# Blocks 8 to 11 normalised in place by GpSimd and transformed in the head; GpSimd issues the stores of x1; last output stores split another way

## The chip, the cores and the metric

The kernel runs on one core of a Trainium2 chip. The core has five engines, each with an instruction stream of its own: TensorE (PE, matmuls; its weight loads are listed as PEld), VectorE (DVE), ScalarE (ACT), GpSimd (POOL) and SyncE (SP, which issues transfers). [...] ACT, SP and POOL issue transfers (DMAs). The metric is the device time of one execution in microseconds; the median of several executions is given.

## The reference, cut to what matters

Two branches are applied to the same normalised input and added to the raw input.

```python
x  = A_u                                   # (1, 2048, 448)
xn = (x - mean(x)) / sqrt(var(x) + 1e-5)   # over the 448 channels
# branch A: a state-space model as a long convolution
dt = exp(log_dt);  A = -exp(log_A_real) + 1j*A_imag;  C = (C_real + 1j*C_imag)*dt
K[d, l] = 2 * Re( sum_n C[d, n] * exp(A[d, n]*dt[d]*l) )     # N = 256, l < 2048
yA = irfft(rfft(K, 4096) * rfft(xn, 4096))[:2048] + xn * D_skip
# branch B: a gated linear unit
yB = (sigmoid(xn @ w_gate) * (xn @ w_up)) @ w_down           # F = 1792
out = x + yA + yB
```

Everything is float32. The kernel writes the matmuls of branch B as three matmuls of rounded parts (high*high, low*high, high*low).

## The kernel before, in words

The 2048 tokens are 16 blocks of 128 tokens (blocks 0 to 7 are the first half, 8 to 15 the second); the 448 channels lie in the free dimension. Two generators write the program: `conv` for branch A and `glu` for branch B. A loop at the end advances whichever is less far, by the estimates in `total`. What they write gets priorities, and when the program is built a scheduler fixes the order on each engine from the dependences, the priorities and its own estimate of when each operand will be there. So a changed line can move instructions far from it. On the chip the order stands.

`conv` has three stages.

1. **Head.** `x_stats` and `x_scales` find mean and inverse root of the variance. `x_scales(sm, 8, 8)` does so for blocks 8 to 15, as a chain of ten small DVE instructions (128x8) after the first guess `ys`. `x_norm` normalises a block. Blocks 0 to 7 are loaded, normalised and transposed at once for the GLU. `x_spec` takes two normalised blocks through the **first Fourier stage**: small matmuls by `wx` (L280) fill three banks of PSUM, `tr`, `ko` and `kp`, which exist once each; three ACT copies (L293 for `tr`, L295 for `ko` and for `kp`) take them to two of three tiles `x1a`, `x1b`, `x1c`, and four DMAs (L300) store these to `x1_d` in DRAM. A bank can be filled again when its copy is done, and a tile when its two DMAs have landed. Beside this `prep` works out the pole parameters from the weights (long DVE and ACT chains, L303 to L430), and the GLU's first feature tiles run.
2. **Kernel spectrum** (`kgen`). For 56 chunks of 8 channels POOL builds magnitudes by doubling (`me`, `mf`, L508 and L520), ACT builds sines `S` (L548 to L551), DVE multiplies them (`Et`, `Ft`, L602 to L604) and PE contracts them (`ko`, L616). A second small transform (L566) stores the spectrum to `sk_d`.
3. **Spectra** (`spectra`). It reads `x1_d` and `sk_d` back, multiplies, transforms back (L902, L929, L962) and adds into the output accumulators; `out` stores these.

`glu` runs the gate and up matmuls (L709), the gate function (`th` on ACT L717, `hf` on DVE L720, `hh` L725, `hl` L727) and the down matmuls (`po`, L825, with the DVE sum L830). It treats blocks 0 to 7 first (half 0) and 8 to 15 after (half 1). PSUM tiles with the tag `gu` exist four times and serve gates, down sums and more. In the last group of half 0, the **cross** stage, the second half's blocks are loaded once more in pairs (`pair_load`); `pair_norm` normalises a pair, `pair_turn` transposes it for the GLU (L213), and `pair_first` puts it through the first Fourier stage: four `gu` banks, four ACT copies (L689), four DMAs on ACT's queue (L691). The table `mid` says which step runs between the two matmul groups of the cross stage's four gates, `end` what follows each gate, and `downs` what follows a down sum:

```python
mid = [(pair_norm, 8), None, (pair_first, 8), (pair_first, 10)]
downs = {(0, 0): (pair_first, 12), (0, 1): (pair_turn, 14), (0, 3): (pair_first, 14)}
```

In the head the second half's blocks also lie in SBUF, raw, in the tiles `xes` (`xe0` for blocks 8 to 11, `xe1` for 12 to 15); before, they serve only `x_stats`, and the space of `xe0` then becomes `p01`.

## Time and profile before

| what | value |
|---|---|
| three timed runs | 711.12, 714.69, 714.64 us |
| median | 714.64 us |
| profiled execution | 710.54 us |
| its span, first to last instruction | 708.8 us |
| mean granted TensorE clock in it | 0.988 |
| PE busy | 668.1 us (94%) |
| DVE, ACT, POOL busy | 555.7, 428.7, 384.9 us |
| DMA traffic | 117.22 MB |

A row of a timeline is: start in us from the span's start, duration in us, engine, line of the kernel, operation, output<-inputs, tile shape, count; in brackets the idle time of that engine just before, and which instruction ended it. ACTq and SPq rows are DMA issues on those queues. A row of a table by stretches gives, for a stretch of time, the busy time of each engine in it, then the granted clock (1.00 is full), the mean busy share of the 16 DMA engines and GB/s.

### The profile page before, as it was taken

To read this page: it belongs to the slowest core of one execution; us is meant where nothing else is said; L and a number is where in the kernel's file an instruction comes from. 1 tells how busy PE (TensorE), PEld (TensorE's weight loads), DVE (VectorE), ACT (ScalarE), POOL (GpSimd) and SP (SyncE) were. 2 spreads that over 40 slices of the span, in tenths; PEclk is the share of its full clock that TensorE was granted. 3 is DMA by queue.
4 is the path that set the end of the run, shared out by engine and by line. 5 is a ranking of instruction groups with operands and counts; after the bars stand their busy time and mean duration, and the time that the engine had idled before them with its cause. 6 is when DMAs were issued, how large, how long until landed. Compare 5 with 4: busy or idle time off the path is not lost. (4 is left out here: it accounts for less than half of the span.)

```text
span 708.8 us, 19098 instructions
## 1 busy us (share of the span) xinstructions
PE 668.1 (94%) x7752; PEld 523.7 (74%) x7752; DVE 555.7 (78%) x766; ACT 428.7 (60%) x678; POOL 384.9 (54%) x433
## 2 busy tenths in 40 slices
PE   2798999999999998999999999999999999999996
PEld 2575878878877875756878878877777777777784
DVE  5899987699899998898478899988946555566544
ACT  3656965578689779877577788778543322322320
POOL 2101227655999999777446698798765001344001
PEclk9999999999999998989999999999999999999999
DMA  9956274554253544546833333242269988999756
GB/s 200 239 149 204 70 230 150 170 183 132 63 169 135 169 123 135 162 146 202 258 112 103 92 112 108 68 138 82 54 179 280 257 236 238 266 272 221 182 146 182
DMA packets 93031, 117.22 MB, mean 165 GB/s; under 512 B 12240, under 2 KB 76624, under 8 KB 92944
## 3 DMA queue, kind: packets, MB, share of 16 engines
q1 hardware_dynamic: 65376, 91.75, 46.3%
q10 hardware_dynamic: 24896, 18.13, 8.7%
q0 software_dynamic: 2672, 6.13, 3.2%
q8 instruction: 61, 1.00, 0.6%
q14 instruction: 26, 0.21, 0.1%
HBM read 72.13 MB, written 43.84 MB: 164 GB/s over the span
## 5 line engine op out<-in xcount | busy, mean ns | idle before, releaser
L520 POOL TENSOR_TENSOR me<-me,pm 128x32 f32<-128x32 f32 (+1 forms) x168 | 154.9, 922 | 66.8 <-DVE Et L603 38.1
L520 POOL TENSOR_TENSOR mf<-mf,pm 128x64 f32<-128x64 f32 (+1 forms) x112 | 116.9, 1044 | 5.1
L709 PE MATMUL gu<-xh,wh 128*128 128x512 f32 x336 | 100.1, 405 | 3.8 <-DVE acc L830 1.6
L709 PE MATMUL gu<-xh,wl 128*128 128x512 f32 x336 | 96.9, 393 | 0.0
L709 PE MATMUL gu<-xl,wh 128*128 128x512 f32 x336 | 95.1, 390 | 0.0
L602 DVE TENSOR_TENSOR Et<-me,S 128x1024 f32<-128x1024 f32 x56 | 80.2, 1433 | 11.6 <-ACT S L551 10.3
L825 PE MATMUL po<-dh,hh 128*128 128x448 f32 x224 | 84.2, 376 | 3.1 <-ACT hh L725 1.9
L548 ACT ACTIVATE S<-tr 128x1024 f32<-128x1024 f32 x56 | 57.7, 1030 | 44.9 <-PE tr L542 41.0
L604 DVE TENSOR_TENSOR Ft<-mf,S 128x1024 f32<-128x1024 f32 x56 | 80.1, 1431 | 5.3 <-PE ko L616 3.7
L603 DVE TENSOR_TENSOR Et<-me,S 128x1024 f32<-128x1024 f32 x56 | 80.4, 1436 | 4.8 <-ACT me L533 4.5
L825 PE MATMUL po<-dh,hl 128*128 128x448 f32 x224 | 82.4, 369 | 0.3 <-DVE hl L727 0.3
L825 PE MATMUL po<-dl,hh 128*128 128x448 f32 x224 | 82.3, 368 | 0.0
L709 PEld LDWEIGHTS gu<-xh,wh 128*128 128x128 f32 x336 | 60.8, 189 | 24.2 <-issue 4.4
L709 PEld LDWEIGHTS gu<-xh,wl 128*128 128x128 f32 x336 | 63.4, 189 | 14.7 <-DVE ve L255 0.7
L709 PEld LDWEIGHTS gu<-xl,wh 128*128 128x128 f32 x336 | 63.0, 188 | 13.5
L725 ACT CAST hh<-hf 128x512 fp32r<-128x512 f32 x56 | 34.9, 623 | 62.4 <-DVE hf L720 61.4
L616 PEld LDWEIGHTS ko<-Et,Ft 128*32 128x32 f32 x3584 | 54.7, 112 | 24.2 <-issue 13.4
L720 DVE SCALAR_TENSOR_TENSOR hf<-th,gu 128x512 f32<-128x512 f32 x56 | 38.1, 680 | 39.9 <-PE gu L709 35.2
L786 POOL TENSOR_TENSOR dl<-rd,dh 128x448 fp32r<-128x448 f32 x14 | 25.6, 1830 | 78.8 <-ACT dh L785 68.5
L616 PE MATMUL ko<-Et,Ft 128*32 128x64 f32 x3584 | 65.2, 223 | 2.6 <-DVE Ft L604 2.4
L551 ACT ACTIVATE S<-S,hpi 128x1024 f32<-128x1024 f32 x56 | 65.5, 1170 | 0.0
L717 ACT ACTIVATE th<-gu 128x512 f32<-128x512 f32 x56 | 33.5, 599 | 49.4 <-PE gu L709 43.0
(208 smaller groups left out, 1318.0 us busy)
## 6 DMA issues: line engine op xcount, KB each, us to landing
sk_d<-sk ACTq DMA_DIRECT2D x14, 512.0 KB
sx<-x_d SPq DMA_DIRECT2D x32, 224.0 KB
skl<-sk_d SPq DMA_DIRECT2D x16, 448.0 KB
vp<-v_d SPq DMA_DIRECT2D x16, 448.0 KB
v_d<-vt SPq DMA_DIRECT2D x14, 448.0 KB
ph<-ph_d SPq DMA_DIRECT2D x224, 24.0 KB
wt_d<-wh SPq DMA_DIRECT2D x9, 512.0 KB
wt_d<-wl SPq DMA_DIRECT2D x9, 512.0 KB
```

The costliest lines, as they stand in the source:

```text
L520: ins = nc.gpsimd.tensor_tensor(m[:, :, w + a : 2 * w : n], m[:, :, a:w:n], par(base + i).unsqueeze(2).to_broadcast([128, 4 * DC, w // n]) ...
L548: nc.scalar.activation(rows(cs), pv, AF.Abs)
L551: sins[:] = [nc.scalar.activation(cs, cs, AF.Sin, scale=-TWO_PI, bias=hpi)]
L602: v.tensor_tensor(Et[:, :, :, 32:64], two(me[:, :, 32:64]), S[:, 1::-1], ALU.mult)
L603: v.tensor_tensor(Et[:, :, :, 0:32], two(me[:, :, 0:32]), S[:, 1:3, :, ::-1], ALU.mult)
L604: fts[:] = [v.tensor_tensor(Ft, two(mf), S[:, 3:5], ALU.mult)]
L616: mm = nc.tensor.matmul(ko[32 * j : 32 * j + 32, sl], Ft[:, cc, DC * h + 4 * q + j], Et[:, cc, DC * h + 4 * q + j], start=(k == 0), stop=( ...
L709: glu_mm[:] = [nc.tensor.matmul(ps, a_, b_, start=(n == 0), stop=(n == len(mm) - 1))]
L717: marks[0] = nc.scalar.activation(th, pgu[0], AF.Tanh, scale=0.5)
L720: marks[1] = v.scalar_tensor_tensor(hf, th, 1.0, pgu[1], ALU.add, ALU.mult)
L725: nc.scalar.copy(hh, hf)
L825: glu_mm[:] = [nc.tensor.matmul(po, a_[:, bs], w_, start=(n == 0), stop=(n == 3 * fc - 1))]
```

## The change

- `x_scales` for blocks 8 to 15: after the first guess the remaining steps run on POOL, as 14 instructions of 128x8, instead of ten on DVE.
- Four POOL instructions (L1088 of the new kernel) then normalise blocks 8 to 11 in place in `xe0`, and two further calls of `x_spec` in the head take them through the first Fourier stage. `p01` takes over the space of `xe0` only after that. The estimate `total` grows by 8.
- `pair_first` for blocks 8 and 10 goes from the cross stage. The pairs are still loaded, normalised and transposed there, for the GLU.
- All stores to `x1_d` (24 DMAs in the head, 8 in the cross stage, 32 as before) are issued by POOL instead of ACT.
- At the end: blocks 12 and 13 are stored in two column halves, the first by POOL before the last stretch; the last stores carry blocks 14 and 15 instead of 15 alone.

```diff
@@ x_scales
+        if b0 >= 8:
+            for _ in range(3):
+                nc.gpsimd.tensor_tensor(z[:, b], y, y, ALU.mult)
+                nc.gpsimd.tensor_tensor(z[:, b], z[:, b], ve[:, b], ALU.mult)
+                nc.gpsimd.tensor_scalar(z[:, b], z[:, b], -0.5, 1.5, ALU.mult, ALU.add)
+                nc.gpsimd.tensor_tensor(y, y, z[:, b], ALU.mult)
+            nc.gpsimd.tensor_tensor(z[:, b], mv[:, b, 0], y, ALU.mult)
+            nc.gpsimd.tensor_scalar(zs[:, b0 : b0 + nb], z[:, b], -1.0, None, ALU.mult)
+            return
@@ x_spec
-                nc.scalar.dma_start(to.rearrange("g i k d -> (i k) g d"), x1s_[p][:, :, H * h : H * h + H])
+                nc.gpsimd.dma_start(to.rearrange("g i k d -> (i k) g d"), x1s_[p][:, :, H * h : H * h + H])
@@ pair_first
-            nc.scalar.dma_start(
+            nc.gpsimd.dma_start(
                 x1_d[:, r : r + 2].rearrange("h i k d -> (i k) h d"), to.rearrange("p (h d) -> p h d", h=2)
@@ glu
-                    mid = [(pair_norm, 8), None, (pair_first, 8), (pair_first, 10)]
+                    mid = [(pair_norm, 8), None, None, None]
...
-                                out(accs[3], 12, 3, slice(0, D), (nc.sync, nc.scalar))
+                                out(accs[3], 12, 2, slice(H, D), (nc.sync, nc.scalar))
...
+                        if final and (t, b) == (1, 1):
+                            out(acc, 12, 2, slice(0, H), (nc.gpsimd,))
...
-                        out(acc, 15, 1, slice(0, D), (nc.sync, nc.scalar))
+                        out(acc, 14, 2, slice(0, D), (nc.sync, nc.scalar))
@@ conv
-                p01 = pst.tile([CP, 2, 2, 2 * N], F32R, name="p01", tag="xe0")
-                for i in range(2):
-                    slots[f"P{i}"] = p01[:, i]
+                for b in range(8, 12):
+                    xe = xes[0][:, b % 4]
+                    nc.gpsimd.tensor_scalar(xe, xe, ys[:, b : b + 1], zs[:, b : b + 1], ALU.mult, ALU.add)
...
+                    if n in (4, 5):
+                        yield from x_spec([xes[0][:, 2 * (n - 4) + i] for i in range(2)], 2 * n)
+                    if n == 5:
+                        p01 = pst.tile([CP, 2, 2, 2 * N], F32R, name="p01", tag="xe0")
@@ the loop that interleaves
-    total = [sum(Y0) + 11 * WP + 8 * WX + 34 + NCK * WK + HOLE + 17 * WS, 2 * (4 + NFT * 14.8) - HELD]
+    total = [sum(Y0) + 11 * WP + 12 * WX + 34 + NCK * WK + HOLE + 17 * WS, 2 * (4 + NFT * 14.8) - HELD]
```

Lines of the new kernel stand 7 lower in the middle (L293, L295, L300 become L300, L302, L307; L709 becomes L716, L825 L832) and up to 16 lower at the end.

POOL in the head, after the load of `sel`: before, two of the GLU's small subtractions `dl` stand there with nothing between them.

```order
L1064 DMA sel<-in_c_sel_dram 128x512
L786 TENSOR_TENSOR dl<-rd,dh 128x448 x2
L584 MEMSET pm_1167 128x128
```

Now (the number behind a name tells tiles of one kind apart) the end of the scale chain, the stores, a `dl` and the four normalisations follow each other there.

```order
L307 DMA x1_d_59<-x1c_480 128x2x224 x2
L261 TENSOR_SCALAR z_87<-z_87 128x8
L307 DMA x1_d_59<-x1ab_383 128x2x224 x2
L262 TENSOR_TENSOR ys_79<-ys_79,z_87 128x8
L793 TENSOR_TENSOR dl_625<-rd_623,dh_622 128x448
L263 TENSOR_TENSOR z_87<-mv_85,ys_79 128x8
L264 TENSOR_SCALAR zs_80<-z_87 128x8
L1088 TENSOR_SCALAR xe0_116<-xe0_116,ys_79,zs_80 128x448 x4
L307 DMA x1_d_59<-x1ab_383 128x2x224 x2
L307 DMA x1_d_59<-x1c_480 128x2x224 x2
```

The stores of the third `x_spec` (the last two rows) now come after the four normalisations, and those of the second in the middle of the chain.

PE in the head: in the new kernel the sixth `x_spec` (`xe0` by `wx`) stands between the last down sum `po` and the next gate, and the order on ACT leads up to the copy of the bank `kp` that the fifth one left (`kp_765`).

```order
L287 MATMUL tr_831<-xe0_116,wx_68 64x448 x4
L287 MATMUL ko_832<-xe0_116,wx_68 64x448 x2
L287 MATMUL kp_833<-xe0_116,wx_68 64x448 x2
L716 MATMUL gu_862<-xh_94,wh_849 128x512 x3
```

```order
L300 COPY x1c_480<-tr_763 128x896
L385 ACT_TABLE_LOAD
L385 ACTIVATE junk_81<-w3_399 112x1
L302 COPY x1ab_383<-ko_764 128x448
L367 ACTIVATE fr_390<-aim_149,hdt_392 112x256 x2
L394 ACTIVATE m3_386<-w3_387,qpi_75 112x512
L395 ACTIVATE s3_388<-w3_387,qpi_75 112x512
L403 CAST ki_389<-fr_390 112x512
L394 ACTIVATE m3_398<-w3_399,qpi_75 112x512
L395 ACTIVATE s3_400<-w3_399,qpi_75 112x512
L302 COPY x1ab_383<-kp_765 128x448
```

Three copies have been put among the activations of `prep`, and the copy of `kp_765` stands behind seven of them; `kp_833` cannot be written before it.

PE in the cross stage, where pair 8 passes its first stage: before,

```order
L542 MATMUL tr<-sel,ph_1112 128x512 x2
L280 MATMUL gu<-xt,wx 64x448 x2
L616 MATMUL ko<-Et_1105,Ft 32x64 x32
L280 MATMUL gu<-xt,wx 64x448 x4
L213 MATMUL gu<-ident,xt 64x128 x2
L542 MATMUL tr<-sel,ph_1112 128x512 x2
L280 MATMUL gu<-xt,wx 64x448 x2
```

and now

```order
L623 MATMUL ko<-Et_1186,Ft 32x64 x27
L716 MATMUL gu<-xl,wh 128x512 x3
L716 MATMUL gu<-xh,wh 128x512 x3
L716 MATMUL gu<-xr,wh 128x512
L716 MATMUL gu<-xh,wl 128x512 x3
L716 MATMUL gu<-xr,wl 128x512
L716 MATMUL gu<-xl,wh 128x512 x3
```

The four groups of small matmuls are gone and gate matmuls follow the chunk directly. Over the whole program the first chunk of `ko` now stands behind 22 more matmuls of the GLU, and the spectra stage begins behind 11 more.

More of the change, by code (lines that the diff above doesn't have):

```diff
@@ L260, in x_scales @@
             v.scalar_tensor_tensor(y, z[:, b], 1.5, y, ALU.add, ALU.mult)
-        neg = lim[:, b0 // 4, 0:1] if b0 < 8 else -1.0
-        v.scalar_tensor_tensor(zs[:, b0 : b0 + nb], mv[:, b, 0], neg, y, ALU.mult, ALU.mult)
-        if b0 < 8:
-            limits(b0 // 4)
+        v.scalar_tensor_tensor(zs[:, b0 : b0 + nb], mv[:, b, 0], lim[:, b0 // 4, 0:1], y, ALU.mult, ALU.mult)
+        limits(b0 // 4)
     def x_norm(xn, xt, b):
@@ L1097, in conv @@
                             yield from x_spec([xns[n - 2][:, b + i] for i in range(2)], 4 * (n - 2) + b)
+                    if n in (4, 5):
+                        yield from x_spec([xes[0][:, 2 * (n - 4) + i] for i in range(2)], 2 * n)
+                    if n == 5:
+                        p01 = pst.tile([CP, 2, 2, 2 * N], F32R, name="p01", tag="xe0")
+                        for i in range(2):
+                            slots[f"P{i}"] = p01[:, i]
             with tc.tile_pool(name="pk", bufs=1, side="right", reuse_waits="tile") as pk:
```

## The prediction

> **What bounds the kernel now.** I read the page first (busy time by engine, granted clock in 40 slices), then a table of busy time by stretches, then groups, waits and timelines of the two stretches that the change touches.

> ```profile
> PE 668.1 (94%) x7752; PEld 523.7 (74%) x7752; DVE 555.7 (78%) x766; ACT 428.7 (60%) x678; POOL 384.9 (54%) x433
> PEclk9999999999999998989999999999999999999999
> 40.00:77.00 37.00, 33.61 (x197) 25.24 (x196) 36.44 (x74) 24.65 (x49) 2.44 (x2) 1.00 0.59 177
> 200.00:270.00 70.00, 67.21 (x1058) 54.62 (x1058) 69.17 (x68) 57.44 (x83) 68.03 (x62) 1.00 0.53 158
> 270.00:290.00 20.00, 18.00 (x243) 11.14 (x241) 16.28 (x18) 17.78 (x30) 18.28 (x20) 0.83 0.43 127
> 290.00:330.00 40.00, 37.31 (x532) 23.68 (x522) 37.05 (x44) 33.80 (x56) 29.88 (x34) 0.91 0.48 152
> 520.00:702.00 182.00, 180.59 (x1553) 137.82 (x1551) 99.05 (x191) 48.74 (x92) 41.57 (x53) 1.00 0.84 226
> ```

> PE is the bound: 668.1 of 708.8 us. Only two things can move the time much: gaps on PE (about 41 us in all) and stretches in which PE runs at a lower clock. From 520 to 702 PE is idle for 1.4 us, so whatever the change shifts there is worth nothing until the last store. The touched places are the head (40 to 77, PE idle 3.4 us, DVE 36.44 of 37) and the cross stage (270 to 330, PE idle 4.7 us, granted clock 0.83 and 0.91). In the 70 us ahead of the cross stage DVE works 69.17 us.

> **Cross stage: what goes.** The groups of PE in 270:290 and 290:300, the clock in steps of 5 us, and two rows of ACT:

> ```profile
> L280 PE MATMUL gu<-xt,wx 32*64 32x448 f32 x16 | 4.7, 663 | 2.0 <-DVE xl L220 1.3 <-DVE hf L720 0.7
> L280 PE MATMUL gu<-xt,wx 32*64 32x448 f32 x16 | 2.0, 560 | 0.0
> 275.00:280.00 5.00, 3.75 (x74) 1.53 (x62) 5.00 (x6) 5.00 (x9) 4.92 (x4) 0.93 0.15 49
> 280.00:285.00 5.00, 5.00 (x73) 3.15 (x73) 3.38 (x3) 5.00 (x9) 4.84 (x7) 0.50 0.56 177
> 285.00:290.00 5.00, 5.00 (x79) 3.79 (x77) 2.90 (x5) 3.24 (x6) 3.83 (x6) 0.89 0.47 142
> 310.00:315.00 5.00, 5.00 (x53) 2.91 (x53) 4.96 (x6) 5.00 (x9) 4.69 (x5) 0.50 0.42 128
> 315.00:320.00 5.00, 5.00 (x71) 3.83 (x70) 4.65 (x6) 3.83 (x7) 0.27 (x2) 0.82 0.27 92
> 301.98 2.77 ACTq L691 DMA_DIRECT2D x_d<-x  x2
> 304.79 0.58 ACT L219 CAST xh<-gu 128x512 fp32r<-128x512 f32 x1 [2.41 <-issue]
> ```

> - Pair 8 takes 4.7 us of PE, pair 10 2.0: 6.7 us of matmul go.
> - Pair 8 waits 2.0 us for free `gu` banks (the releasers are DVE's `xl` and `hf`). These waits go with it, unless DVE is itself the limit.
> - The clock: after these small, waiting matmuls it is 0.93, 0.50 and 0.89 in three steps of 5 us, a loss of (0.07 + 0.50 + 0.11) x 5 = 3.4 us. Some 0.9 of it is already in the 4.7 (the last group of pair 8 took 1.75 us instead of 0.97 in the timeline), so 2.5 us more. I take it as gone, since pair 8's stalls precede it. A second such stretch (310 to 320, again (0.50 + 0.18) x 5 = 3.4 us) follows pair 12's first stage, which stays; I leave it.
> - Sum: 6.7 + 2.0 + 2.5 = 11.2 us at the most. Against it stands DVE: in 270 to 330 it is busy 16.28 + 37.05 = 53.3 of 60 us, so if every step there needs DVE, no more than its idle 6.7 us can go. If DVE's backlog from before 270 carries on, still less: 0 to 3. I take **−8** (0 to −11): above DVE's 6.7 because part of the removed matmuls stood where PE, not DVE, was full (280 to 290, DVE 6.28 of 10).
> - ACT's two store issues at 301.98 took 2.77 us and left ACT 2.41 us without work; these go to POOL, which is idle 10 us in 290 to 330 and gets eight issues. With one more row,

> ```profile
> L239 POOL DMA_DIRECT2D out_dram<-ac x8: 551/551/563, 639.1 to 643.0; - x8
> ```

> eight at 0.55 are 4.4 us: hidden, if no `me`/`mf` step that DVE waits for is behind them. Price without that cover: 4.4 us. I count 0.

> **Head: what comes.** PE at full width, ACT, and the nearest POOL rows:

> ```profile
> 41.02 0.60 PE L280 MATMUL tr<-xn,wx 32*64 32x448 f32 x4
> 41.96 0.96 PE L709 MATMUL gu<-xh,wh 128*128 128x512 f32 x3
> 76.81 0.86 PE L709 MATMUL gu<-xh,wh 128*128 128x512 f32 x3
> 46.63 1.20 SPq L642 DMA_DIRECT2D wraw<-in_B_w_up_dram  x2
> 50.71 1.05 ACT L759 CAST wh<-wraw 128x1024 fp32r<-128x1024 f32 x1 [1.11 <-DMA wraw<-in_B_w_up_dram]
> 62.85 1.19 SPq L642 DMA_DIRECT2D wraw<-in_B_w_up_dram  x2
> 66.03 0.89 ACT L293 COPY x1ab<-tr 128x896 f32<-128x896 f32 x1
> 68.90 0.53 ACT L295 COPY x1ab<-ko 128x448 f32<-128x448 f32 x1
> 79.83 0.71 ACT L388 ACTIVATE s<-w,qpi 112x512 f32<-112x512 f32 x1
> 80.45 0.61 ACT L396 CAST ki<-fr 112x512 int32<-112x512 f32 x1
> ```

> An `x_spec` costs PE 0.94 us (41.02 to 41.96, sixteen matmuls side by side), so two cost 1.9 us. But the sixth stands in front of the gates that started at 76.81, and its bank `kp` is free only when ACT has copied the fifth's. On ACT that copy now stands just behind the last `prep` activation, which ended at 80.45. To that time come: a third wide copy (0.8), two narrow ones (0.95), a cast that now stands earlier (0.5), so 82.7 less 0.5 that starts overlap = 82.2. Two waits are ahead of it on the same engine. A cast of the next weights `wh` has been moved ahead of the activations; its load is issued at 62.85, and the earlier such load was cast 4.1 us after its issue (46.63 to 50.71, with 1.11 us of waiting), so it can start near 66.95: about 0.9 us of waiting. And the copies into the tile `x1ab` wait for the stores of its last content, which POOL issues only after the four normalisations: about 0.7. So the copy starts near 83.8, ends near 84.3, and the gates start near 84.5 instead of 76.81: **+7.7**. Without the waits it is +6.1. If the activations run earlier than I think, because ACT is ahead, only the matmuls stay: +1.9. All prices of the normalisation hang on POOL:

> ```profile
> 47.38 0.17 DVE L256 TENSOR_SCALAR ys<-ve 128x8 int32<-128x8 int32 x1
> 112.88 0.32 POOL L508 TENSOR_TENSOR mf<-GG,pm 128x64 f32<-128x64 f32 x1
> 119.23 1.29 POOL L520 TENSOR_TENSOR mf<-mf,pm 128x64 f32<-128x64 f32 x1
> 84.11 4.41 POOL L786 TENSOR_TENSOR dl<-rd,dh 128x448 fp32r<-128x448 f32 x1 [24.74 <-ACT dh L785]
> L793 POOL CAST dh<-rdw x5: 551/552/791, 513.1 to 643.5; 128x448 fp32r<-128x448 f32 x5
> ```

> The trace has no 128x8 instruction of POOL. The nearest are 128x64: 0.32 us alone and 1.29 beside a busy DVE. Fourteen are 4.5 to 18.1 us; I take 0.6 each, 8.4, since DVE's instructions in the head are mostly shorter than the `Et` that runs beside the 1.29. The four normalisations have one tensor operand, as the cast of the same shape has (0.55), so 2.2 us, and at most 4 x 4.41 = 17.6 by the two-operand `dl`. With twelve issues ahead of them (6.6) POOL's share is some 17 us from 47.4 on, done near 65 to 70. The fifth and sixth stages are then not late, as the gates in question come after 76. DVE is spared ten instructions of about 0.1 us, 1 us; it is full here, but PE waits for ACT, so 0.

> [...]

> [...]

> ```profile
> 35.35 0.50 PE L709 MATMUL gu<-xr,wh 128*128 128x512 f32 x1 [2.53 <-DVE xr L226]
> 61.25 0.47 PE L825 MATMUL po<-dh,hh 128*128 128x448 f32 x1 [1.85 <-ACT hh L725]
> ```

> The longest gaps of the head, 2.53 and 1.85 us, left the clock at 1.00. The new one is longer: 7.7 − 1.9 leaves 5.8 us of idle PE, of which some 1.5 to 2 lies ahead, where copies of the fifth stage hold PE too, so 3.7 to 4.4 in one piece. I leave its clock out of the forecast and put it into the slow rival.

> **Tail.**

> ```profile
> L239 SPq DMA_DIRECT2D out_dram<-acc x6: 316/674/980, 701.1 to 704.6; - x6
> 699.41 2.21 DVE L970 TENSOR_TENSOR acc<-acc,pv 128x448 f32<-128x448 f32 x4 [0.34 <-PE pv L962]
> 702.00:709.00 7.00, 0.09 (x1) 0.00 (x0) 0.62 (x1) 0.00 (x0) 0.00 (x0) 0.78 0.66 196
> ```

> After the last matmul six issues on SP's queue and six on ACT's put out 7 us x 196 GB/s = 1.37 MB. Half of blocks 12 and 13 (2 x 128 x 224 x 4 bytes = 0.23 MB) now leaves earlier: 0.23 MB at 196 GB/s is 1.2 us at most, and nothing if the last blocks' own landing sets the end. I take **−0.7**. The early half is issued by POOL, 0.55 us; POOL is busy 41.6 of 182 us there, so it is hidden.

> The spectra's later start (11 more matmuls ahead of them) changes no sum while PE is busy 180.59 of 182 us. Price if they starve: the 11 matmuls by 0.4 us, 4.4.

> **Sum.** 710.54 + 7.7 − 8 − 0.7 = 709.5. The profiled execution lies 0.6 us under the lowest of the three runs and 4.1 under their median; two runs stand at 714.7 and one at 711.1, a step of 3.5 us, as large as one of the clock losses above. A changed kernel may show either level; I add 1: **710.5 us**. Against the median of 714.64 that is faster by 0.6%, at the edge of what a measurement of this kernel can tell from no change (about 0.5%, 3.6 us).

> **Rivals.**

> 1. *The head costs more: POOL's chain is late (718).* If DVE holds POOL up in each of the fourteen small steps, as at 119.23, the stores of tile `x1c`, which POOL issues behind ten of them, are reached at 47.4 + 10 x 1.29 = 60.3.

> ```profile
> rdw<-in_B_w_down_dram POOLq DMA_DIRECT2D x5, 224.0 KB, 4.3
> 60.58 0.62 ACT L725 CAST hh<-hf 128x512 fp32r<-128x512 f32 x1 [2.64 <-DVE hf L720]
> ```

> Two issues (1.1) and a landing as that of `rdw`, which POOL issues too (4.3), make 65.7. ACT's copy of the third stage (0.9) waits for that tile, and the `hh` behind it starts near 66.8 to 67.2 instead of 60.58, 6.6 later. ACT's two waits of the forecast (1.6) and some 1.2 of its other idle time (12.3 of 37 us) take up 2.8 of that: the head costs 7.7 + 3.8 = 11.5, and the gap on PE, over 4 us, lowers the clock: 3.4 more. 710.5 − 7.7 + 11.5 + 3.4 = 717.7. It decides from 0.65 us a step: 60.4, where ACT needs the tile, less 47.6, 1.1, 4.3 and 0.9 leaves 6.5 for ten. For it: DVE is 98% busy in 40 to 77. Against: its instructions there differ from those beside the 1.29.
> 2. *The cross stage gives all (704.5).* The whole 11.2, the second clock loss too (half of 3.4) and no waits in the head (+6.1): 711.5 + 6.1 − 11.2 − 1.7 − 0.7 = 704. For it: both clock losses follow a first stage that waits, and DVE has idle time after 280. Against: DVE is full before 275, and pair 12 stays.
> 3. *The change gives nothing there.* DVE is the limit of the cross stage, the gain there is 3, the head floor 6.1: 711.5 + 6.1 − 3 − 0.7 = 713.9, no difference.

> **How the numbers follow.** Forecast 0.45, its own range 707 to 714 (the gain between 6.7 and 10, the head between 6.1 and 9); the slow head 0.22, the full gain 0.25, the third 0.08. Half of the forecast's case lies under 711.1, which is faster by over 0.5%: 0.45 x 0.46 + 0.25 = 0.46 faster. Over 718.2 is most of the slow head and a little of the rest: 0.19. The remaining 0.35 is within. The range, 703 to 719, takes in the full gain and the slow head, and leaves out both clock losses gone with a free head, and a slow head with a full DVE.

> **What would show it.** In the profile of the changed kernel: the gates after the sixth `x_spec` start near 84.5, with a wait of `kp` for ACT's copy of 3.7 to 4.4 us ahead; POOL's fourteen steps take 0.3 to 0.65 us each; the clock is 1.00 from 275 to 290 (times shifted by the head); PE's groups in the cross stage hold 32 matmuls of L287 fewer; the last store lands some 5 us after PE's last matmul. It is wrong if `kp` waits under 2 us, if a clock step follows it, if the cross stage of the new kernel takes as long as before, or if PE waits there for POOL.

## The result, and the profile after

The changed kernel takes **733.71 us** (median of five: 737.20, 732.91, 732.34, 733.71, 734.04), the kernel before 712.79 (five, 710.22 to 714.69). The ratio is 1.0299, with an interval of 1.0269 to 1.0330: 3% slower, where the prediction had 710.5 and a range up to 719. The profiled execution of the changed kernel is the 737.20 one, with a span of 735.4 us; before it was 708.8. The two profiled executions thus lie 26.6 us apart, the medians 20.9: nearly 6 us of what the traces below add up to are this pair's own spread.

The same two lines of the page as before, then the table of busy time by stretches:

```profile
PE 679.0 (92%) x7752; PEld 532.5 (72%) x7752; DVE 568.3 (77%) x756; ACT 428.3 (58%) x676; POOL 414.9 (56%) x487
PEclk9998899999998999998999999999999999999999
40.00:77.00 37.00, 35.15 (x188) 23.54 (x188) 35.61 (x64) 21.51 (x46) 28.13 (x36) 0.91 0.53 169
77.00:100.00 23.00, 20.23 (x91) 14.95 (x90) 18.90 (x31) 20.17 (x38) 7.59 (x9) 0.85 0.49 153
200.00:270.00 70.00, 63.15 (x919) 51.41 (x918) 57.52 (x61) 51.02 (x73) 53.36 (x55) 0.95 0.43 134
300.00:350.00 50.00, 40.58 (x616) 27.78 (x613) 44.62 (x49) 37.85 (x60) 43.22 (x55) 0.90 0.44 134
350.00:540.00 190.00, 181.45 (x2747) 148.28 (x2749) 167.74 (x161) 135.23 (x194) 148.71 (x158) 0.98 0.36 107
540.00:726.00 186.00, 183.83 (x1684) 140.97 (x1681) 104.24 (x191) 53.74 (x99) 43.98 (x57) 0.99 0.82 221
```

PE has the same number of matmuls, 10.9 us more busy time and 15.7 us more idle time; together that is the 26.6 us by which the spans differ. The added busy time is not added work: weighting each slice's busy time with its granted clock gives 662.3 us of work at full clock, against 661.3 before. So some 16 us went to gaps and 10 us to half clock; the 1 us more of work is within the error of this weighting.

That weighting also gives a ruler. If the busy time times the clock is added up along each trace, both kernels can be compared at the same amount of PE work done. The table shows how many us later than the kernel before a kernel reaches that point (all worked out from slices of 2.5 us, one trace for each kernel; the last three rows are experiments, told below):

| PE work done (us) | 40 | 90 | 190 | 210 | 250 | 270 | 310 | 330 | 470 | 650 |
|---|---|---|---|---|---|---|---|---|---|---|
| time of the kernel before | 57 | 111 | 212 | 233 | 275 | 299 | 346 | 366 | 509 | 691 |
| changed kernel | −0.1 | +6.6 | +6.2 | +13.2 | +13.1 | +13.3 | +15.8 | +16.0 | +24.3 | +26.5 |
| changed, interleaved as before | +2.2 | +5.2 | +5.0 | +5.4 | +5.9 | +3.0 | +7.5 | +10.9 | +10.1 | +10.7 |
| the same, accumulator loads later | +0.2 | +6.5 | +6.2 | +5.4 | +5.7 | +3.1 | +6.2 | +6.2 | +5.3 | +6.1 |
| before, with the new `total` alone | 0.0 | +0.2 | +0.4 | +6.0 | +8.3 | +8.4 | +6.9 | +6.9 | +9.7 | +11.9 |

The changed kernel loses 6.6 us in the head, 7 us in one piece between 220 and 246 us of its own time, 3 over the cross stage, 8 in the second half of the kernel spectrum, and 2 in the spectra. (The +2.2 in the second kernel's first column is half clock from 34.2 to 41.0 us, behind 2.08 us of idle time from 30.8 to 34.2, ahead of the steps that were added; see the last section.) Only the first of these stands in the sum of the prediction.

**The head.** Waiting PE rows, ACT's copy that releases one of them, and the chain on POOL:

```profile
60.91 0.73 PE L287 MATMUL ko<-xn,wx 32*64 32x448 f32 x2 [1.85 <-ACT x1c L302]
85.71 1.76 PE L287 MATMUL kp<-xe,wx 32*64 32x448 f32 x4 [2.77 <-ACT x1ab L302]
85.14 0.51 ACT L302 COPY x1ab<-kp 128x448 f32<-128x448 f32 x1
48.01 5.48 POOL L261 TENSOR_SCALAR z<-z 128x8 f32<-128x8 f32 x1
54.42 1.28 POOL L261 TENSOR_SCALAR z<-z 128x8 f32<-128x8 f32 x1
56.82 1.49 POOL L307 DMA_DIRECT2D x_d<-x1c  x2 [0.28 <-issue]
64.25 3.62 POOL L1088 TENSOR_SCALAR xe<-xe,ys,zs 128x448 f32<-128x448 f32 x4
60.00:65.00 5.00, 4.09 (x13) 2.28 (x14) 5.00 (x7) 2.29 (x8) 4.78 (x6) 0.62 0.62 197
85.00:90.00 5.00, 4.29 (x10) 2.41 (x11) 4.39 (x8) 4.94 (x10) 1.63 (x3) 0.51 0.30 97
```

`kp` waits for ACT's copy as foreseen, and the third stage's `ko` waits for a copy whose tile `x1c` is stored from the middle of POOL's chain, which is the slow rival's place. But the idle time of the head grew by 0.4 us only; the rest, some 6.2 us, is half clock, 6.8 us long each, behind these two gaps.

**The stall near 226 us.** Rows of POOL, SP, ACT and PE in order of time:

```profile
221.39 5.78 POOL L527 TENSOR_TENSOR mf<-mf,pm 128x64 f32<-128x64 f32 x4
227.13 1.19 POOL L793 TENSOR_TENSOR dl<-rd,dh 128x448 fp32r<-128x448 f32 x1
228.34 0.34 SPq L796 DMA_DIRECT2D dt_d<-dl  x1
229.26 3.33 SPq L499 DMA_DIRECT2D ph<-ph_d  x8
231.59 0.40 ACTq L581 DMA_DIRECT2D sk_d<-sk  x1
232.09 1.02 ACT L555 ACTIVATE S<-tr 128x1024 f32<-128x1024 f32 x1 [9.81 <-DMA ph<-ph_d]
234.57 1.22 PE L549 MATMUL tr<-sel,ph 128*128 128x512 f32 x2 [6.27 <-ACT S L557]
```

ACT's copies of `sk` are done at 222.3, and the store of `sk` is issued at 231.6. Why it waits for a load of `ph`, which has nothing to do with it, is seen in the program's order with its waits (SP's first `ph` load, and ACT's store):

```
L499 DMA ph1_1194<-ph_d_58 12x2x256 [waits DMAHW2_49,PE_49]
L581 DMA sk_d_60<-sk_1181 128x8x128 [waits DMAHW2_49,Activation_49]
```

In this program the transfers of SP and ACT take eight semaphores in turn (in the trace, the numbers 100, 101 and 110 to 115), and by the waits listed with them one that takes a semaphore again waits until its last user has landed. The store's last user is a `ph` load that SP issues behind the store of `dl`, at 229.26, 2.33 us ahead of the store; `dl` stands on POOL behind 5.8 us of `mf`. Nothing behind the store runs on ACT in these 9.81 us. So GpSimd holds up SP, SP holds up ACT, ACT holds up PE, which stands 6.27 us.

**The tail.** PE's last matmul started at 729.21 of 735.4 us, before at 701.72 of 708.8; with 0.37 us for each, 5.8 us follow it instead of 6.7.

### The profile page after: what moved, and what is told of

Its sections match the earlier page's. It is cut to its first block, busy times and chain, and to the rows that moved or that the text cites. A ratio compares the mean times of both kernels' runs of the same rounds, so it can differ in the third digit from the quotient of the medians.

```text
span 735.4 us, 19134 instructions
## 1 busy us (share of the span) xinstructions
PE 679.0 (92%) x7752; PEld 532.5 (72%) x7752; DVE 568.3 (77%) x756; ACT 428.3 (58%) x676; POOL 414.9 (56%) x487
## 5 line engine op out<-in xcount | busy, mean ns | idle before, releaser
L527 POOL TENSOR_TENSOR me<-me,pm 128x32 f32<-128x32 f32 (+1 forms) x168 | 146.5, 872 | 61.0 <-ACT pm L464 42.1
L527 POOL TENSOR_TENSOR mf<-mf,pm 128x64 f32<-128x64 f32 (+1 forms) x112 | 122.0, 1089 | 4.0
L716 PE MATMUL gu<-xh,wh 128*128 128x512 f32 x336 | 101.8, 409 | 2.1 <-DVE xl L220 0.9
L716 PE MATMUL gu<-xh,wl 128*128 128x512 f32 x336 | 98.0, 398 | 0.0
L610 DVE TENSOR_TENSOR Et<-me,S 128x1024 f32<-128x1024 f32 x56 | 87.9, 1569 | 10.8 <-ACT me L540 7.4
L716 PE MATMUL gu<-xl,wh 128*128 128x512 f32 x336 | 96.1, 393 | 0.0
L832 PE MATMUL po<-dh,hh 128*128 128x448 f32 x224 | 86.1, 384 | 2.8 <-DVE acc L837 2.8
L609 DVE TENSOR_TENSOR Et<-me,S 128x1024 f32<-128x1024 f32 x56 | 77.8, 1389 | 14.0 <-ACT S L558 12.7
L611 DVE TENSOR_TENSOR Ft<-mf,S 128x1024 f32<-128x1024 f32 x56 | 82.1, 1466 | 2.9 <-PE ko L623 2.4
L832 PE MATMUL po<-dh,hl 128*128 128x448 f32 x224 | 84.0, 376 | 0.0
L832 PE MATMUL po<-dl,hh 128*128 128x448 f32 x224 | 83.8, 374 | 0.0
L716 PEld LDWEIGHTS gu<-xh,wh 128*128 128x128 f32 x336 | 61.8, 192 | 22.8 <-issue 5.4
L623 PEld LDWEIGHTS ko<-Et,Ft 128*32 128x32 f32 x3584 | 54.9, 111 | 30.2 <-issue 11.1
L716 PEld LDWEIGHTS gu<-xh,wl 128*128 128x128 f32 x336 | 64.3, 192 | 14.9 <-DVE ve L255 0.7
L716 PEld LDWEIGHTS gu<-xl,wh 128*128 128x128 f32 x336 | 63.7, 190 | 13.8
L837 DVE SCALAR_TENSOR_TENSOR acc<-po,acc 128x448 f32<-128x448 f32 x80 | 48.4, 616 | 21.0 <-PE po L832 20.9
L734 DVE TENSOR_TENSOR hl<-hf,hh 128x512 fp32r<-128x512 f32 x56 | 48.5, 865 | 15.3 <-ACT hh L732 15.2
## 6 DMA issues: line engine op xcount, KB each, us to landing
sx<-x_d SPq DMA_DIRECT2D x32, 224.0 KB
```

What stands on the lines that cost most here:

```text
L527: ins = nc.gpsimd.tensor_tensor(m[:, :, w + a : 2 * w : n], m[:, :, a:w:n], par(base + i).unsqueeze(2).to_broadcast([128, 4 * DC, w // n]) ...
L609: v.tensor_tensor(Et[:, :, :, 32:64], two(me[:, :, 32:64]), S[:, 1::-1], ALU.mult)
L610: v.tensor_tensor(Et[:, :, :, 0:32], two(me[:, :, 0:32]), S[:, 1:3, :, ::-1], ALU.mult)
L611: fts[:] = [v.tensor_tensor(Ft, two(mf), S[:, 3:5], ALU.mult)]
L623: mm = nc.tensor.matmul(ko[32 * j : 32 * j + 32, sl], Ft[:, cc, DC * h + 4 * q + j], Et[:, cc, DC * h + 4 * q + j], start=(k == 0), stop=( ...
L716: glu_mm[:] = [nc.tensor.matmul(ps, a_, b_, start=(n == 0), stop=(n == len(mm) - 1))]
```

## The experiments

### Who issues the stores

```diff
@@ x_spec and pair_first: of the changed kernel, back to ScalarE (first run); of the kernel before, to GpSimd (second)
-nc.gpsimd.dma_start(x1_d ...)
+nc.scalar.dma_start(x1_d ...)
```

> The changed kernel with one part undone: ScalarE issues all stores to x1_d again. The changed kernel's median is 733.7 us, before it 712.8. Theory P (the loss comes from GpSimd having these 32 issues in its stream: each took 0.73 us there, and they hold up the GpSimd steps that DVE, SP and PE wait for) expects 715 to 724, no 6 us stall near 226, and no wait of the third stage's copy in the head. Theory O (the loss comes from the moved first stages: more work in the head, another order of everything behind it, and a clock that halves after each gap) expects 727 to 737, with the wait of kp in the head of about 2.8 us and the half clock after it.

> The kernel before with one part done alone: GpSimd issues all stores to x1_d, nothing else. Theory P expects 718 to 726 (32 issues of 0.73 us, those of the cross stage ahead of GpSimd steps that DVE waits for). Theory O expects 709 to 715, within 0.5% of before, since GpSimd has room in the head and ScalarE is relieved by as much.

Measured: 737.82 us, ratio to before 1.0315 (1.0282 to 1.0347), and 719.26 us, 1.0065 (1.0037 to 1.0094). Giving the stores back to ScalarE brings nothing, and the 6.2 us stall of `tr` is there too: theory P falls. Theory O's sign in the head was not quite met either: `kp` waits 1.74 us, and a down sum waits 5.64 us for GpSimd's `dl`, so the head costs 10.4 us instead of 6.6. GpSimd's issues alone do cost 5 us in the kernel before, but the trace puts this down to one place and not to their number. That kernel is within 2 us of before up to 345 us and loses the time at one place:

```profile
352.44 0.32 ACTq L243 DMA_DIRECT2D acc<-in_A_u_dram  x1
352.86 0.62 ACT L725 CAST hh<-hf 128x512 fp32r<-128x512 f32 x1 [12.03 <-DMA acc_d<-acc]
355.39 1.94 PE L616 MATMUL ko<-Et,Ft 128*32 128x64 f32 x64 [5.86 <-DVE Ft L604]
```

ACT stands 12 us at the load of the second half's accumulators, which waits until the first half's have been stored; in the kernel before it stands 5.75 us there. DVE's `Ft` comes late by it, and PE stands 5.9 us. No run was made of GpSimd's issues with this wait removed. This place comes back below.

### What the removal is worth

```diff
@@ glu, of the kernel before (first run)
-mid = [(pair_norm, 8), None, (pair_first, 8), (pair_first, 10)]
+mid = [(pair_norm, 8), None, None, None]
@@ glu, of the changed kernel (second run): the reverse
```

> The kernel before without the first stage of blocks 8 to 11 in the cross stage, which is left out (their rows of x1_d get those of blocks 0 to 3, by eight more stores that GpSimd issues in the head). It measures what the removal is worth by itself. The prediction's theory expects 703 to 707 (a gain of 6 to 10: 6.7 of matmuls, 2 of waits, a halved clock less). The rival, that DVE is the limit of the cross stage, expects 710 to 713 (0 to 3).

> The changed kernel with the first stage of blocks 8 to 11 done a second time in the cross stage, where it was before. If the removal is worth 6 to 10 us in the changed kernel, as predicted, this takes 740 to 744. If DVE is the limit there, 733 to 737. The distance to the kernel before is then what the head, the issues by GpSimd and the new order cost without any gain.

Measured: 710.55 us, ratio 0.9965 (0.9940 to 0.9989), and 744.77 us, 1.0426 (1.0400 to 1.0451). The first run leaves out the first stage of blocks 8 to 11 and stores that of blocks 0 to 3 in its place; the eight more stores cost no time that the trace shows (−0.8 us at a work of 90). By itself the removal gives the kernel before 2.5 us (from the ratio), near the rival in which DVE is the limit. In the changed kernel it is worth 9 us by the ratios (1.0426 to 1.0299). Both cannot be the same amount of removed waiting: its worth depends on what stands around it. And without any gain the rest of the change costs 30 us, four times what the prediction put down for it.

### The interleaving

```diff
@@ the loop that interleaves, of the kernel before (first run); the reverse in the changed kernel (second run)
-total = [sum(Y0) + 11 * WP + 8 * WX + ...
+total = [sum(Y0) + 11 * WP + 12 * WX + ...
```

> The kernel before with only the estimate total of the change (12 first stages): the same work in another order. If order alone makes losses of that size, 718 to 730. If before's order is no better than its neighbours, 709 to 716.

> The changed kernel with the estimate total as before (8 first stages instead of 12), so that the two branches are interleaved otherwise, with the same work. If the later losses (225, 455, 525, 660 us: some 17 us) hang on how far GLU and kernel spectrum have got against each other, the time moves by 5 us or more, either way, and the stall near 226 is gone or elsewhere. If they hang on the moved work itself, 731 to 736.

Measured: 725.07 us, ratio 1.0175 (1.0126 to 1.0225), and 737.37 us, 1.0349 (1.0303 to 1.0395). The first is the plainest finding of the study: the kernel before, with not one instruction added, removed or given to another engine, is **12 us slower** for an estimate that is 8 larger. The first chunk of the kernel spectrum runs in two pieces; the second, the first to run in one piece, then stands behind 453 matmuls of the GLU instead of 464, later ones mostly behind 2 to 28 fewer. (The 22 more that are told ahead of the prediction are this chunk's too; the first one starts behind 9 more.) The last row of the table above shows where the time goes: 5.6 us between 212 and 239 us, the rest in small steps up to 560. At that place two operands come late, and the clock is halved from 225.4 to 232.2 us:

```profile
223.33 0.27 PE L566 MATMUL kp<-wk,ks 64*64 64x64 f32 x1 [1.41 <-POOL ks L627]
227.16 1.94 PE L616 MATMUL ko<-Et,Ft 128*32 128x64 f32 x64 [3.15 <-DVE Ft L604]
```

In the changed kernel the old value is no cure, since the two added first stages also count as progress of branch A: there 497 matmuls stand ahead of the second chunk, and the losses lie elsewhere. So time is lost with fewer matmuls ahead of the chunk than 464 and with more.

So the next run takes both away: `total` as before, and the added stages count for nothing.

```diff
@@ conv, the loop that interleaves, of the changed kernel
-                        yield from x_spec([xes[0][:, 2 * (n - 4) + i] for i in range(2)], 2 * n)
+                        for _ in x_spec([xes[0][:, 2 * (n - 4) + i] for i in range(2)], 2 * n):
+                            pass
-total = [sum(Y0) + 11 * WP + 12 * WX + ...
+total = [sum(Y0) + 11 * WP + 8 * WX + ...
```

> The changed kernel with the two branches interleaved as before: the two added first stages are not counted as progress (they yield nothing) and total has its old value. On PE the first chunk of the kernel spectrum then stands behind 464 matmuls of the GLU, as before, instead of 486. Theory O2 (the head costs some 6.6 us, the cross stage gains some 7 to 11, and the remaining 15 to 20 us of loss come from the shifted interleaving alone) expects 711 to 719, no stall near 226 us and none of the later half clocks. If the later losses come from the moved work or GpSimd's issues, 725 to 735.

Measured: 722.80 us, ratio 1.0129 (1.0081 to 1.0177). 464 matmuls stand ahead of the second chunk as before (372 instead of 399 ahead of the first, and small differences in the cross stage remain), and of the 21 us of loss 11 are gone. By the table's second kernel, the stall near 226 us and all losses from 370 us on have gone with it, while GpSimd still issues and normalises everything. It is not as fast as theory O2 had it: the cross stage's gain (5.9 to 3.0) is given back, and more (10.9).

Two variants of it:

> As the run before this one (interleaving as before) and ScalarE issues the stores to x1_d. GpSimd's issues alone cost the kernel before 5 us in the cross stage; if they cost the same here, this is 3 to 6 us faster than with GpSimd's issues: 706 to 715. If the head's waits on ScalarE's queue take that back, the same as it within 2 us.

> As the run before this one, and DVE does the scale chain and the four normalisations too, so that GpSimd has no new instruction in the head. If GpSimd's chain (13 us from 47 to 61 us, and four normalisations behind it) brings on the first gap of PE in the head and its half clock (1.85 and 3.2 us), this is 3 to 6 us faster than with it: 702 to 710. If DVE, which is full from 40 to 77 us, passes its longer work on to PE, it is no faster: 706 to 716.

Measured: 724.40 us, 1.0145 (1.0097 to 1.0192), and 721.08 us, 1.0111 (1.0054 to 1.0167). Neither the issuer nor the engine of the normalisation decides. In the second, GpSimd has nothing new in the head, and no time is lost up to 90 us, but it then loses 8 us from 111 to 180 us, where the first stages have been moved by the scheduler.

### The stall near 226 us

```diff
@@ first_stage, of the changed kernel
-            nc.scalar.dma_start(sk_to, tl["sk"]...)
+            nc.gpsimd.dma_start(sk_to, tl["sk"]...)
```

> The changed kernel with the 14 stores of the kernel spectrum (sk_d) issued by GpSimd instead of ScalarE. Near 226 us ScalarE stood 9.8 us at such a store: the order shows that it waits for the eighth transfer before it, a load of ph that SP issues only after a store that waits for GpSimd's dl. If that chain holds PE up, the 6.3 us stall of tr and the half clock behind it (8 us together) go: 725 to 729 less what 14 issues of about 0.6 us cost GpSimd (0 to 8). If the stall is due to ph itself, tr waits for ph instead, and the time stays at 732 to 738.

Measured: 742.52 us, ratio 1.0437 (1.0372 to 1.0503). The 6.3 us stall at this place is gone, as the chain SP to ACT says: at a work of 210 us the kernel is 6.4 us behind the kernel before, not 13.2. But GpSimd passes the time on 6 us later:

```profile
244.81 0.47 PE L832 MATMUL po<-dl,hh 128*128 128x448 f32 x1 [3.74 <-POOL dl L793]
258.17 1.10 PE L623 MATMUL ko<-Et,Ft 128*32 128x64 f32 x64 [2.58 <-DVE Et L609]
```

The chain through the shared semaphore was the way that the stall took; its source is that `dl` comes late on GpSimd against the GLU's place.

### The loads behind the cross stage

In the kernel with before's interleaving 6.6 us are lost between 329 and 377 us. The first 3.3 of them, up to 344 us, are lost with a gap of 2.0 us and half clock from 331 to 338; the rest follows this place:

```profile
348.01 1.22 SPq L846 DMA_DIRECT2D acc_d<-acc  x1
354.49 2.20 ACTq L243 DMA_DIRECT2D acc<-in_A_u_dram  x4
356.73 0.62 ACT L732 CAST hh<-hf 128x512 fp32r<-128x512 f32 x1 [9.50 <-issue]
```

The same wait as above: ACT stands 9.5 us until the accumulators that SP stored at 348.0 have landed. In the kernel before it stands 5.75 us, ahead of a `th`:

```profile
347.40 0.60 ACT L717 ACTIVATE th<-gu 128x512 f32<-128x512 f32 x1 [5.75 <-DMA acc<-in_A_u_dram]
```

The loads were put behind the second and fourth gate of the second half.

```diff
@@ glu
-                    x_load(accs[q], 4 * q, 4, [nc.scalar])
...
+                    if half == 1 and fs_ is ORDER[1][0] and n_ in (1, 3):
+                        q = n_ // 2 + 2
+                        with tc.issue_after(marks[0].ins):
+                            x_load(accs[q], 4 * q, 4, [nc.scalar])
```

> The kernel before with ScalarE's loads of the second half's accumulators put behind two and four gates of that half. In the kernel before ScalarE stands 5.75 us at the second set of loads; if PE is not held by that there, 711 to 715, no change. If it is, 706 to 710.

> The kernel before without the first stage of blocks 8 to 11 in the cross stage (left out, as in the earlier run: 710.6) and with ScalarE's loads of the accumulators later. If the wait at these loads takes back what the shorter cross stage gains (4 us at 300 us, none at 366), this is 703 to 707. If DVE's backlog takes it back, 709 to 713.

> The changed kernel with the interleaving of before (722.8) and with ScalarE's loads of the accumulators later. The wait there was 9.5 us, and the loss against before grew by 6.6 us between 325 and 377 us. If that wait is the cause, 715 to 719. If the gaps of the cross stage itself are (2.85 of 5 us busy at 310, 3.29 at 330, and half clocks behind both), 721 to 724.

Measured: 710.95 us, ratio 0.9961 (0.9939 to 0.9982); 706.06 us, 0.9894 (0.9866 to 0.9922); 719.70 us, 1.0077 (1.0052 to 1.0102). The kernel before gains 0.4% by it, and so is **faster than both kernels of this case**. With the loads out of the way the removal is worth 4.8 us there (0.9961 to 0.9894) instead of 2.5, and the changed kernel gets 3 to 4 us back, between what the two sides of the last expectation asked for. So a part of the gain was indeed given back at this wait: a shorter cross stage only brought ACT to it sooner. The table's third kernel is 5.7 us behind at a work of 250, 3.1 at 270 and 6.2 from 310 on, flat to the end: what is left is the head, and a cross stage that gains 3 us and loses them again.

### The head and the half clock

> The changed kernel with redundant matmuls (the wide bank of the same first stage is written three or four times more, with the same values) in the two gaps that PE has in the head ahead of ko of the third and kp of the sixth first stage (1.85 and 2.77 us). It adds about 3.5 us of work where PE was idle. If the half clock from 60 to 70 and from 85 to 95 us is brought on by these gaps, it goes, and about 6.2 us with it: 726 to 729, clock 1.00 from 60 to 100. If the half clock has another cause (the load of the engines, the mix of matmuls), it stays and the time is 733 to 738.

```diff
@@ x_spec, of the changed kernel
             for j in range(4):
+                for _ in range({(4, 2): 3, (10, 3): 4}.get((b0, j), 0)):
+                    for i in range(2):
+                        x_first_stage(ps[:, i, :D], xn, i)
                 x_first_stage((ps[:, j] if j < 2 else kk[j - 2])[:, :D], xn, j)
```

Measured: 740.63 us, ratio 1.0400 (1.0352 to 1.0448). It tells little: ACT's order changed, the third stage's `tr` now waited 5.8 us for ACT, with three windows of half clock behind it, and everything after came late enough for `kp` not to wait. A filled gap was not shown.

> The changed kernel with the interleaving of before, and GpSimd runs one small tensor_scalar of the kind in the scale chain some 30 us earlier, on values that are overwritten later. In the chain the first such instruction took 5.48 us, the second 1.28, the third 0.69. If the 5.48 is a cost of the first use, the early one takes about 5 us and the chain's first about 1; the chain ends 4 to 5 us earlier, the stores that stand in it go out earlier, and the head loses 1 to 3 us less: 719 to 722. If it is DVE that holds GpSimd up, the early one is short, the chain's first stays long, and the time is 722 to 725.

```diff
@@ x_scales, of the kernel interleaved as before
+        if b0 == 0:
+            nc.gpsimd.memset(zs[:, 8:16], 1.0)
+            nc.gpsimd.tensor_scalar(zs[:, 8:16], zs[:, 8:16], -0.5, 1.5, ALU.mult, ALU.add)
```

Measured: 722.58 us, 1.0122 (1.0098 to 1.0146), the same as without it (722.80). In this trace the chain's first step of the kind takes 0.51 us, but so it does in the trace of the kernel without the early instruction:

```profile
49.37 0.51 POOL L264 TENSOR_SCALAR z<-z 128x8 f32<-128x8 f32 x1
50.27 0.51 POOL L261 TENSOR_SCALAR z<-z 128x8 f32<-128x8 f32 x1
```

(the first row with it, the second without). So the 5.48 is no price of a first use, and the other theory is left. Rows of DVE in the changed kernel fit it:

```profile
52.74 0.69 DVE L323 SCALAR_TENSOR_TENSOR pl<-pl,fr 112x514 f32<-112x514 f32 x1
53.35 1.75 DVE L329 RECIPROCAL m<-m 112x128 f32<-112x128 f32 x2
```

GpSimd's step of 5.48 us starts at 48.01 and ends at 53.49, while DVE works without a break, mostly on instructions with two tensor operands, until the reciprocal at 53.35; the next one (1.28) ends at 55.70, again just after a reciprocal starts (55.57). In nine of the eleven traces with this chain one of its first three steps takes 4.8 to 5.5 us, whichever its form; in the other two GpSimd got in between DVE's instructions at about 0.5 us each. That DVE shuts GpSimd out there is what the rows suggest; a run that takes DVE's work away was not made. What it did to PE is open. The two kernels here, without the long step, are 2.2 and 1.8 us late at a work of 40 already, and lose 3.0 and 3.7 from there to 90: the sixth stage waits 1.3 and 0.9 us near 79 us, and half clock follows. The kernel with the later loads (above) has the long step, the same waits of the sixth stage, and one of 1.77 us for the third stage's `ko` with half clock behind it; it loses 6.3. That fits a price of some 3 us, but the orders of ACT and PE differ a little there too.

> The changed kernel with the interleaving of before and the later accumulator loads (719.7), with redundant matmuls (the wide bank of the sixth first stage is written again with the same values) ahead of that stage's ko and kp. PE was idle 1.31 and 0.86 us there and ran at half clock from 82 to 89 us (3.3 us lost). If the gaps bring on the half clock, it goes: 715.5 to 717.5. If they do not, the added work costs and the half clock stays: 720 to 723.

> The kernel before with the later accumulator loads (711.0) and with redundant matmuls (a bank is written again with the same values) between the second and third group of the first stages of pairs 8 and 12 in the cross stage, where PE waited for banks and the half clock followed (3.4 us each). If the gaps that they fill bring on the half clock, 704 to 709. If the gaps ahead of the first groups do, which they don't fill, 711 to 714.

```diff
@@ first: x_spec as in the diff with the fill above, with {(10, 2): 2, (10, 3): 3}; second: pair_first
             x_first_stage(pss[g][:, :D], xns, g)
+            for _ in range(2 if g == 1 and b % 4 == 0 else 0):
+                x_first_stage(pss[g][:, :D], xns, g)
```

Measured: 728.71 us, ratio 1.0231 (1.0197 to 1.0264), and 717.87 us, 1.0078 (1.0051 to 1.0106). Both are slower than without the fill and than either theory allowed. The first decides nothing: in its trace ACT's copies come later, and PE stands 4.72 us, up to 92.7 us, for one of them, a wait that was not there before. In the second the theory that busy matmuls keep the clock up fails (a PE row, and two stretches that each are one step of the clock, below):

```profile
276.41 3.19 PE L280 MATMUL gu<-xt,wx 32*64 32x448 f32 x16
276.70:280.10 3.40, 3.40 (x20) 1.19 (x16) 3.40 (x5) 3.40 (x6) 3.32 (x3) 1.00 0.06 20
280.10:283.50 3.40, 3.40 (x58) 1.62 (x60) 3.04 (x3) 3.40 (x8) 3.24 (x5) 0.50 0.42 140
```

PE is busy without a break for 3.4 us, and the clock halves all the same; the added matmuls are some 3.5 us of work besides. What fills the time are matmuls of 32 rows by 64 columns, which start two at a time, 0.37 us apart; whether that is why the clock halves is not shown. Their shape alone did not do it: in the first fill of this section the same matmuls ran four at a time over such a step, and full clock followed:

```profile
91.47 2.06 PE L287 MATMUL tr<-xe,wx 32*64 32x448 f32 x20
91.60:95.00 3.40, 3.40 (x44) 1.37 (x35) 3.40 (x7) 0.88 (x2) 0.00 (x0) 1.00 0.43 137
95.00:98.40 3.40, 3.26 (x16) 2.42 (x15) 2.61 (x5) 2.34 (x5) 0.00 (x0) 1.00 0.47 133
```

So the half clock in the kernel before at 279 us, which the prediction put down to pair 8's stalls, may be due to its small matmuls too: its step ahead, from 275.9 us, has 1.25 us of idle time, and the small matmuls in it also run two at a time. No run separates the two.

### The tail

```diff
@@ glu, of the kernel before
-out(accs[3], 12, 3, slice(0, D), (nc.sync, nc.scalar))
+out(accs[3], 12, 2, slice(H, D), (nc.sync, nc.scalar))
...
+if final and (t, b) == (1, 1):
+    out(acc, 12, 2, slice(0, H), (nc.gpsimd,))
...
-out(acc, 15, 1, slice(0, D), (nc.sync, nc.scalar))
+out(acc, 14, 2, slice(0, D), (nc.sync, nc.scalar))
```

> The kernel before with the new split of the last stores alone. The prediction says 0.7 us faster (0 to 1.1). If it is not the split but the landing of the very last blocks that sets the end, 0. A change of order elsewhere would show as more than 2 us either way.

Measured: 713.68 us, ratio 0.9990 (0.9963 to 1.0017): no difference that shows. In its trace 5.7 us follow the last matmul, before 6.7, so the split does what it should.

## Why the prediction was wrong, point by point

- **What bounds the kernel** was right: PE, its gaps and its clock. From that followed, wrongly, that shifted work is worth nothing. The prediction looked for this in the spectra alone, where PE is full and 11 later matmuls do cost nothing. The shift by 22 matmuls at the start of the kernel spectrum is shown ahead of the prediction and has no term in it. **This is the step that failed**: some 11 us (733.7 to 722.8), and 12 for the same estimate in the kernel before. PE is busy for 97% of 100 to 520 us in the one order of the kernel before; in the other orders GpSimd's `dl` or `ks`, DVE's `Ft` or a load comes 1 to 6 us late here and there. Why these orders do so and that one does not is left open.
- **Head, +7.7.** Measured +6.2 to +6.6. Right in place, wrong in kind, and in size by luck: `kp` waited 2.77 us (3.7 to 4.4 forecast), part of which replaced idle time that was there before, and the half clock behind the two gaps made 6.2 us. The forecast left the clock out and gave it to the slow rival, with the reason that gaps of 2.53 and 1.85 us had left it at 1.00. That reason does not hold (last section). That a gap of over 4 us lowers the clock, a further 3.4 us in the slow rival, no trace of before shows; in the changed kernel 6.8 us of half clock followed each of the gaps of 1.85 and 2.77 us (6.2 us lost together) and the one of 6.27 us near 228. GpSimd's fourteen small steps took 11.1 us instead of 8.4 (half of it the one of 5.48, which fits the slow rival: DVE holds GpSimd up), its four normalisations 3.6 instead of 2.2, an issue of a store 0.73 instead of 0.55; with that the slow rival's mechanism, the late store of `x1c`, took place, at 1.85 us of PE instead of 6.6, and half clock behind it.
- **Cross stage, −8.** Mis-sized. The removal by itself is worth 2.5 us, 4.8 with the wait for the accumulators out of the way. The 6.7 us of matmuls counted at their stretched duration, and the half clock was counted as removed although pairs 12 and 14 keep the same small matmuls, and it came back: in the changed kernel for 3.4 us from 303.6, behind a step with 2.3 us of idle PE, and for 6.8 us from 337.7, behind pair 14; with the interleaving of before, half clock cost 6.3 to 7.2 us from 300 to 340 us in three traces, as much as the two half clocks of the kernel before together (6.8). The wait of ACT behind the stage was visible in the profile of before (5.75 us) and was not looked at.
- **GpSimd as issuer, 0** was right for the changed kernel (giving it back: 737.8 against 733.7, and 724.4 against 722.8). In the kernel before it costs 5 us, by its trace at the same wait for the accumulators.
- **Tail, −0.7.** Some −0.9 in the traces, within the bounds and too small for the times to show.
- **The rivals.** The slow one (718) was the right sign, by a mechanism that made a small part of the loss. None had the order as its mechanism. (A slip: the second rival's terms add up to 704.0, not 704.5.)

So of the 23 us between forecast and measurement (733.7 and 710.5) some 11 are the order, 3 the wait at the accumulator loads (722.8 to 719.7), and 8 the forecast gain of the cross stage, of which the table's third kernel has nothing left from a work of 310 on.

The changed kernel with order and accumulator loads mended is still 0.8% behind the kernel before (1.2% behind it with the same loads moved, 719.7 to 711.0), flat from the head on but for the cross stage. What a head without these two gaps would make of it was not reached: of three attempts the early GpSimd instruction changed nothing, and DVE for GpSimd and the fill moved the loss elsewhere.

## What to carry to other kernels

Where a planner's estimate sets how two branches interleave, a change that adds to the estimate is two changes: try the same estimate without the work (here +12 us), and the work without the estimate (here −11), before crediting the work with anything. Work that leaves a stage only pays up to the next wait with a fixed date: look for what the engines stand at directly behind the shortened stage (here a load that waits for a store), and move that first. And compare two traces at equal work done on the bounding engine, not at equal time: the jumps then point to a few places.

## What was not expected of the hardware

| PE idle in the step of 3.41 us | steps | of these with half clock next |
|---|---|---|
| 1.8 us and more | 69 | 68 |
| 1.2 to 1.8 | 67 | 18 |
| 0.6 to 1.2 | 184 | 10 |
| less than 0.6 | 3569 | 7 |

Each of the seven in the last row lies in a step with 1.4 to 3.1 us of first-stage matmuls; some 40 steps of this row have as much, so these matmuls alone do not decide it. Steps of the changed kernel, the first, third and fourth with half clock behind them, the second not:

```profile
57.80:61.20 3.40, 1.55 (x12) 0.40 (x12) 3.40 (x5) 0.88 (x3) 3.34 (x6) 1.00 0.62 202
272.90:276.30 3.40, 2.44 (x31) 1.67 (x31) 3.40 (x3) 2.61 (x4) 3.40 (x3) 1.00 0.32 86
453.80:457.20 3.40, 1.49 (x65) 1.00 (x67) 3.40 (x3) 3.40 (x5) 3.32 (x3) 1.00 0.16 41
525.40:528.90 3.50, 0.98 (x5) 0.56 (x3) 3.50 (x2) 0.82 (x1) 3.22 (x3) 0.99 0.00 0
```

So in these traces a gap's length tells less than its share of a step; between 1.2 and 1.8 us the idle time alone does not tell (18 of 67). The gap of 2.5 to 2.8 us near 33 us, which every trace has, fell on two steps in the kernel before (1.08 and 1.76 us of idle time) and left the clock alone, as in the nine other traces in which no step there has more than 1.76; in the ten in which one step has 2.08 to 2.76 half clock follows. In the changed kernel the gap of 1.85 us cost 3.4 us of clock (6.8 us at half), and the 1.91 us of idle time in the step from 453.8 cost 1.7; the gap of 2.53 us in the kernel before cost nothing. The grid does not start with the kernel: its first step after 15 us begins between 15.2 and 18.2 us in the 20 traces. By the author's estimate (half of 3.41) this could move the time from one execution to the next by steps of 1.7 us; it was not shown, for each kernel was traced once.

Also new: the transfers issued by SP and ACT share eight semaphores in turn in this program (100, 101 and 110 to 115 in the trace of the changed kernel), so that a store on ACT can wait for an unrelated load on SP (9.8 us at one place); whoever moves transfers between queues also changes which transfer waits for which.
